# Asking for the first queries and keys ahead of every other transfer, in a scheduled attention and experts kernel

## The chip, the cores and the metric

The kernel runs on one core of a Trainium2 chip, as one program. The metric is the time of one execution in microseconds of device time, as the median of several runs; lower is better. The engines have short names: PE multiplies matrices, DVE, ACT and POOL are the vector, scalar and GpSimd engines, SP issues most of the transfers. Each engine runs its own list of instructions in order, and waits at an instruction for semaphores that others raise.

## What is computed

```python
def _attn_ref(q, k, v):                       # 4 batches, 8 heads, 576 rows, head size 64
    scores = scale * np.matmul(q, k.transpose(0, 1, 3, 2))
    kth = np.partition(scores, -32, axis=-1)[..., -32:-31]
    scores = np.where(scores >= kth, scores, -1e9)
    attn = softmax(scores)
    return np.matmul(attn, v)

def _moe_ref(x, modality_id, w_gate, modality_bias, w1, w2):   # 2304 tokens of 512
    e_idx = np.argmax(x @ w_gate + modality_bias[modality_id], axis=1)
    out[e_idx == e] = gate_w * (np.maximum(x @ w1[e], 0.0) @ w2[e])

def _moe2_ref(x, w_in, w_out, g_ln):          # w_in and w_out come as float64
    h = x @ w_in
    ln = layernorm(h * softmax(h)) * g_ln
    return ln @ w_out
```

Attention keeps the 32 largest scores of each row. Every token then goes to one of 8 experts, and after that through a dense block whose two weight matrices arrive as float64 numbers.

## The kernel before

**The work.** Attention goes through 4 batches of 5 query tiles: four of 128 rows and a short one of 64 (`t == 4`). Within a tile it goes through four pairs of heads. One head of one tile is a *unit* (a whole head pair for the short tile); there are 144. In a unit PE makes scores (L579), ACT copies them (L600, L610), DVE finds the 32nd largest with a run of maximum and replace steps (L612 to L629), ACT and POOL mask and take the exponential (L647 to L651). A `pair` then transposes the weights and multiplies them by the values (L664 to L742). After a tile, `route` and `place` count the tokens of each expert and scatter their numbers into a list in device memory, `idlist`, with an indirect transfer from POOL (L817). An expert slot (`front`, `back`) picks an expert, gathers token numbers (L884) and rows (L893), loads the expert's weights (L942, L945) and runs 128 tokens through them (L984, L1015); `moe2` does the dense block (L1036 to L1108).

**The float64 weights** come in 16 pieces. `doubles` loads one (L345) and rebuilds it as a float32 value and a remainder: ACT L346 and L355, POOL L348 and L357, DVE L349, L351 and L353. Three workers (`statics`) do this while attention runs. `consts` loads the token kinds, biases and gate weights (L294 to L301).

**What sets the order.** All of it is written as Python generators, which a small list scheduler (`Order`) plays at build time. A generator yields an `Op` (engine, assumed cost, the function that emits the instructions), a `get` or `put` of buffers, a `set` of an event, or an event that it waits for. The scheduler keeps a clock for each engine, picks the engine that can go first, and among the operations ready there the one with the best priority from the table `PRI`. So each engine's list of instructions is fixed when the program is built, and a small difference at its start can move many later choices. Nothing in the scheduler is a wait at run time; those are semaphores that the framework adds where one instruction needs another's result or buffer. An `Ev` is met once its time is set:

```python
        if isinstance(x, Ev):
            if x.t is None:
                return False
```

`load_k` asks for the keys of one head pair at a time (three transfers, L470 and L471, assumed cost 1900), `load_q` for the queries of a tile (L483, 530). Each has two buffers to begin with. `prep_kv` and `prep_q` transpose what has landed (L515, L522, L541) and split it in two parts (L490, L491). For a short query tile `prep_q` first writes zeros to two quarters of the tile with POOL (two instructions at L552).

Of the kernel before, what the change touches and what calls it, by code (L numbers as in the profile page):

```python
# [63 lines left out]
def tiles(b):  # L64


    return (4, 0, 1, 2, 3) if b < SHORT_FIRST else (0, 1, 2, 3, 4)


def rows_of(b, t):  # L70

    if t == 4:
        return (0 if b < SHORT_FIRST else 512), 64
    return t * 128 + (64 if b < SHORT_FIRST else 0), 128
# [125 lines left out]
def attn_moe_solu_kernel(ctx, tc, q, k, v, mid, w_gate, mbias, w1, w2, w_in, w_out, g_ln, out):  # L200
# [56 lines left out]
    def bc(ap, n, axis):  # L257
        shape = list(ap.shape)
        u = ap.unsqueeze(axis)
        shape.insert(axis, n)  # L260
        return u.to_broadcast(shape)
# [9 lines left out]
    def consts():  # L271


        yield "get", ("row", 2), ("xs", 1), ("B", 1)
        ta, tb = [sb.tile([128, NP * 144], F32, tag="row", name="cs", bufs=BUF["row"]) for _ in range(2)]
        tc_ = sb.tile([128, NP, 144], F32, tag="xs", name="cs", bufs=BUF["xs"])
        zl, bias2 = ta[:, 0:NLIST // 128].bitcast(I32), ta[:, 160:160 + B * NTILE * E].rearrange("p (i e) -> p i e", e=E)
        raw, rows = tb[0:32, 0:256].bitcast(I32), tb[0:64, 256:384]
        b01 = tc_[:, 0, 0:2 * E].rearrange("p (m e) -> p m e", e=E)
        mids = tc_[:, 1, 0:64]  # L280
        m32 = mid.bitcast(I32).rearrange("(n w) -> n w", w=2)

        def clear():
            nc.vector.memset(zl, 0)
            nc.vector.memset(raw, 0)
            nc.vector.memset(rows, 0.0)
            nc.vector.memset(iw, 0.0)

        yield Op("DVE", 1200, clear)

        def loads():
            for b in range(B):
                o4, o0 = b * S + rows_of(b, 4)[0], b * S + rows_of(b, 0)[0]
                nc.sync.dma_start(raw[4 * b:4 * b + 4, :], m32[o0:o0 + 512].rearrange("(t p) w -> t (p w)", p=128))  # L294
                nc.sync.dma_start(raw[4 * B + b:4 * B + b + 1, 0:128], m32[o4:o4 + 64].rearrange("(t p) w -> t (p w)", p=64))
            nc.sync.dma_start(rows[32:40, :], g_ln.rearrange("(k p) -> k p", p=128))
            nc.sync.dma_start(b01, bass.AP(tensor=mbias.tensor, offset=mbias.offset, ap=[[0, 128], [E, 2], [1, E]]))
            wgv = w_gate.rearrange("(p s d) e -> s d p e", s=2, d=D)
            for s in range(2):
                nc.sync.dma_start(iw[s * D:(s + 1) * D, :, 136 * s:136 * s + 8], wgv[s])  # L300
            nc.sync.dma_start(idlist.rearrange("(p c) o -> p (c o)", p=128), zl)  # L301

        t0 = yield Op("SP", 700, loads, lat=10000)

        def unit_rows():
            for s in range(2):
                r = slice(s * D, (s + 1) * D)
                nc.vector.tensor_copy(iw[r, :, 8 + s * D:8 + (s + 1) * D], bc(ident[r, s * D:(s + 1) * D], NP, 1))

        yield Op("DVE", 650, unit_rows, deps=[])  # L310
        yield Op("POOL", 330, lambda: nc.gpsimd.tensor_copy(rows[0:32], raw.rearrange("i (n w) -> i n w", w=2)[:, :, 0]), deps=[t0])
        pt = ps.tile([128, 64], F32, tag="B", name="pt", bufs=8)
        yield Op("PE", 60, lambda: nc.tensor.transpose(pt, rows, ident[0:64, 0:64]))
        yield Op("ACT", 250, lambda: nc.scalar.activation(mids, pt, AF.Copy))
        yield "put", ("B", 1)

        def biases():
            m, n = mids[:, 0:B * NTILE], mids[:, 32:32 + B * NTILE]
            nc.gpsimd.tensor_copy(g_sb, mids[:, 32:40])
            nc.gpsimd.tensor_scalar(n, m, -1.0, 1.0, op0=OP.mult, op1=OP.add)  # L320
            nc.gpsimd.tensor_tensor(bias, bc(n, E, 2), bc(b01[:, 0, :], B * NTILE, 1), op=OP.mult)
            nc.gpsimd.tensor_tensor(bias2, bc(m, E, 2), bc(b01[:, 1, :], B * NTILE, 1), op=OP.mult)
            nc.gpsimd.tensor_tensor(bias, bias, bias2, op=OP.add)

        yield Op("POOL", 1700, biases)
        yield "put", ("row", 2), ("xs", 1)
        yield "set", consts_done
# [125 lines left out]
    def after(n):  # L453
        if n:
            yield units_done[n]

    kraw, qraw = {}, {}
    k_loaded = {(b, p): Ev() for b in range(B) for p in range(NP)}
    q_loaded = {(b, t): Ev() for b in range(B) for t in range(NTILE)}

    def load_k():

        for b in range(B):
            for p in range(NP):
                yield "get", ("kr", 1)
                kr = kraw[b, p] = sb.tile([128, 10, D], F32, tag="kr", name="kr", bufs=BUF["kr"])

                def loads():
                    for s in range(2):
                        nc.sync.dma_start(kr[:, s:8:2, :], k[b, 2 * p + s, 0:512].rearrange("(p c) d -> p c d", c=4))  # L470
                    nc.sync.dma_start(kr[0:64, 8:10, :], k[b, 2 * p:2 * p + 2, 512:576, :].rearrange("s p d -> p s d"))  # L471

                t0 = yield Op("SP", 1900, loads, deps=[], lat=0)
                k_loaded[b, p].t = t0 + 3000
                yield "set", Ev()

    def load_q():
        for b in range(B):
            for t in tiles(b):
                r0, n = rows_of(b, t)  # L480
                yield "get", ("qr", 1)
                qr = qraw[b, t] = sb.tile([128, H, D], F32, tag="qr", name="qr", bufs=BUF["qr"])
                t0 = yield Op("SP", 530, lambda: nc.sync.dma_start(qr[:n], q[b, :, r0:r0 + n, :].rearrange("h p d -> p h d")),  # L483
                              deps=[], lat=0)
                q_loaded[b, t].t = t0 + 3000
                yield "set", Ev()

    def parts_of(hi, lo, pt, n):

# [745 lines left out]
    def statics(j):  # L1235

        steps = [(static_w_in, kk, i) for kk in range(KD) for i in range(2)]
        steps = ([(static_w_out, kk) for kk in range(KF)] + steps) if OUT_FIRST else (steps + [(static_w_out, kk) for kk in range(KF)])
        if j == 0:
            yield "get", ("xs", 1)  # L1240
            minus.append(sb.tile([128, NP * 144], F32R, tag="xs", name="minus", bufs=BUF["xs"])[:, 0:128])
            yield Op("ACT", 170, lambda: nc.scalar.activation(minus[0], ident, AF.Copy, scale=-1.0))
        for i in range(j, len(steps), WORKERS):
            yield from after(STATIC[i])
            yield from steps[i][0](*steps[i][1:], j)
        yield "set", in_done[j]
        if j == 0:
            yield from static_centre()
            for e in in_done:
                yield e  # L1250
            yield "put", ("xs", 1)
            yield "set", statics_done
# [158 lines left out]
    with tc.manual_schedule():  # L1411
        ord_.add(load_k(), pri("prep", 0))
        ord_.add(load_q(), pri("prep", 0))
        ord_.add(consts(), pri("const", 0))
        ord_.add(prep_k_all(), pri("prep", 0))
        ord_.add(prep_q_all(), pri("prep", 1))
        ord_.add(attention(), pri("unit", 0))
        for i in range(WORKERS):
            ord_.add(statics(i), pri("static", 0))
        ord_.add(slots(), pri("front", 0))  # L1420
        ord_.add(backs(), pri("ffn", 1))
        ord_.add(remains(), pri("ffn", 2))
        ord_.run()
# [60 lines left out]
```

## Time and profile before

| | us |
|---|---|
| median of 3 runs | 1048.77 |
| lowest and highest run | 1045.49, 1050.99 |
| the profiled execution | 1044.1 |
| its span, first to last instruction | 1042.3 |
| PE busy | 922.2 (88%) |
| DVE busy | 783.1 (75%) |
| ACT busy | 671.3 (64%) |
| POOL busy | 595.2 (57%) |

The shares are means over stages with different limits: DVE works nearly all the time while attention runs, to about 808 us, and little after it. Three views serve here. The windows view gives each engine's busy time in a stretch. The timeline lists instructions with their start and duration, and in brackets the idle time before one and what ended it. The chain of waits goes back from the last instruction to what released each step. A transfer appears with its issue on SPq or POOLq, or as a duration to its landing in the chain.

### The profile page before, as it was taken

To read this page: it belongs to the slowest core of one execution; us is meant where nothing else is said; L and a number is where in the kernel's file an instruction comes from. 1 tells how busy PE (TensorE), PEld (TensorE's weight loads), DVE (VectorE), ACT (ScalarE), POOL (GpSimd) and SP (SyncE) were. 2 spreads that over 40 slices of the span, in tenths; PEclk is the share of its full clock that TensorE was granted. 3 is DMA by queue.
4 is the path that set the end of the run, shared out by engine and by line. 5 is a ranking of instruction groups with operands and counts; after the bars stand their busy time and mean duration, and the time that the engine had idled before them with its cause. 6 is when DMAs were issued, how large, how long until landed. Compare 5 with 4: busy or idle time off the path is not lost.

```text
span 1042.3 us, 22339 instructions
## 1 busy us (share of the span) xinstructions
PE 922.2 (88%) x7150; PEld 758.6 (73%) x7150; DVE 783.1 (75%) x2474; ACT 671.3 (64%) x1688; POOL 595.2 (57%) x1334
## 2 busy tenths in 40 slices
PE   3867759998989899999999999999999989998983
PEld 2434536976768788787887878888788778887872
DVE  5999969997799999789999898999999224432001
ACT  3767748776677778777777778877776523433211
POOL 4667856656456776657486675666774536541201
PEclk7788878999999999999999999999999999999997
DMA  6524153544414354554444445344444566433440
GB/s 164 167 68 134 49 89 96 162 116 99 127 52 116 93 155 84 148 129 125 131 114 74 145 112 118 96 129 94 119 123 83 78 158 192 136 108 103 150 125 14
DMA packets 153752, 119.28 MB, mean 114 GB/s; under 512 B 48508, under 2 KB 126488, under 8 KB 153624
## 3 DMA queue, kind: packets, MB, share of 16 engines
q1 hardware_dynamic: 149528, 107.69, 40.1%
q0 software_dynamic: 4096, 10.05, 3.1%
q8 instruction: 59, 0.97, 0.4%
q14 instruction: 69, 0.57, 0.2%
HBM read 105.50 MB, written 12.21 MB: 113 GB/s over the span
## 4 chain that ended last, share of the span: by engine, by line
PE 41%; DVE 17%; POOL 9%; DMA 7%; ACT 7%; issue 5%; SPq 0%; POOLq 0%; ACTq 0%; DVEq 0%
PE py L1015 8%; PE ph L984 7%; PE po L1097 7%; DMA wraw<-in_moe_w_dram 5%; PE ph L1036 5%; DVE M L620 4%; PE po L717 4%; POOL e L649 3%; PE pt L683 3%; PE pS L579 2%; DVE tht L629 2%; PE pt L914 2%; PE px L726 1%; DVE M L612 1%; ACT e L648 1%
## 5 line engine op out<-in xcount | busy, mean ns | idle before, releaser
L649 POOL TENSOR_TENSOR e<-ss,e 128x576 f32<-128x576 f32 x144 | 204.7, 1424 | 51.7 <-ACT e L648 46.3
L984 PE MATMUL ph<-xT,wraw 128*128 128x128 f32 x1088 | 149.6, 282 | 9.7 <-DMA wraw<-in_moe_w_dram 9.5
L1015 PE MATMUL py<-hh,wraw 128*128 128x128 f32 x1088 | 148.6, 281 | 7.4 <-ACT hh L994 6.5
L984 PEld LDWEIGHTS ph<-xT,wraw 128*128 128x128 f32 x1088 | 136.4, 196 | 16.2 <-DMA wraw<-in_moe_w_dram 7.1
L651 ACT ACTIVATE e<-e,nb 128x576 f32<-128x576 f32 x144 | 111.6, 775 | 52.6 <-POOL e L649 51.3
L1015 PEld LDWEIGHTS py<-hh,wraw 128*128 128x128 f32 x1088 | 134.9, 195 | 13.3 <-ACT hh L994 8.3
L648 ACT ACTIVATE e<-ss,bt 128x576 f32<-128x576 f32 x144 | 111.2, 774 | 38.4 <-POOL bt L647 38.2
L620 DVE MATCH_REPLACE8 M<-tops,M 128x288 f32<-128x288 f32 x288 | 127.2, 443 | 0.0
L1097 PE MATMUL po<-wo,lT 128*128 128x512 f32 x432 | 119.9, 415 | 4.5 <-DVE lT L922 2.2
L717 PE MATMUL po<-eT,vt 128*64 128x128 f32 (+3 forms) x1600 | 116.5, 280 | 7.0 <-ACT eT L687 4.1
L1036 PE MATMUL ph<-wi,yT 128*128 128x512 f32 x432 | 115.1, 407 | 2.0 <-ACT yT L1203 1.9
L717 PEld LDWEIGHTS po<-eT,vt 128*64 128x64 f32 (+1 forms) x1600 | 84.0, 140 | 40.1 <-issue 15.5
L629 DVE MAX8 tht<-M 128x8 f32<-128x576 f32 x144 | 107.9, 750 | 0.6
L579 PE MATMUL pS<-kT,qT 64*128 64x288 f32 (+1 forms) x864 | 94.2, 322 | 13.5 <-ACT kT L490 5.0
L683 PE MATMUL pt<-identr,e 128*128 128x128 f32 (+1 forms) x640 | 95.3, 274 | 9.7 <-ACT wi L382 6.6
L687 ACT ACTIVATE eT<-pt 128x512 f32<-128x512 f32 (+1 forms) x160 | 88.1, 551 | 15.0 <-PE pt L683 13.0
L579 PEld LDWEIGHTS pS<-kT,qT 64*128 64x128 f32 (+1 forms) x864 | 72.1, 192 | 31.2 <-issue 8.2
L1097 PEld LDWEIGHTS po<-wo,lT 128*128 128x128 f32 x432 | 77.7, 192 | 23.1 <-DVE lT L922 4.2
L683 PEld LDWEIGHTS pt<-identr,e 128*128 128x128 f32 (+1 forms) x640 | 72.4, 144 | 26.3 <-issue 7.3
L1036 PEld LDWEIGHTS ph<-wi,yT 128*128 128x128 f32 x432 | 76.5, 188 | 20.2 <-ACT yT L1203 2.8
L994 ACT ACTIVATE hh<-ph 128x128 f32<-128x128 f32 (+1 forms) x144 | 40.1, 278 | 71.3 <-PE ph L984 63.4
L612 DVE TENSOR_TENSOR M<-pS,ss 128x288 f32<-128x288 f32 x144 | 64.5, 448 | 24.8 <-ACT ss L610 24.0
(218 smaller groups left out, 1819.6 us busy)
## 6 DMA issues: line engine op xcount, KB each, us to landing
wraw<-in_moe_w_dram SPq DMA_DIRECT2D x288, 256.0 KB
xrows<-xs SPq DMA_DIRECT2D x16, 288.0 KB
kr<-in_k_dram SPq DMA_DIRECT2D x32, 128.0 KB
qr<-in_q_dram SPq DMA_DIRECT2D x16, 256.0 KB
raw<-in_moe_w_out_dram SPq DMA_DIRECT2D x8, 512.0 KB
vt<-in_v_dram SPq DMA_DIRECT2D x32, 128.0 KB
raw<-in_moe_w_in_dram SPq DMA_DIRECT2D x8, 512.0 KB
wstage<-da SPq DMA_DIRECT2D x8, 256.0 KB
```

The costliest lines, as they stand in the source:

```text
L579: nc.tensor.matmul(bank[s][hf], x[r, a, p, :], kt[r, c, at:at + HALF], start=i == 0, stop=i == 2)
L620: nc.vector.match_replace(out=M, in_to_replace=rounds[r], in_values=M, imm_value=NEG)
L629: t0 = yield Op("DVE", 660, lambda: nc.vector.max(th, W), deps=[t0, tm])
L648: yield Op("ACT", 667, lambda: nc.scalar.activation(e, ss, AF.Relu, bias=bt, scale=-BIG))
L649: yield Op("POOL", 1360, lambda: nc.gpsimd.tensor_tensor(e, ss, e, op=OP.subtract))
L651: yield Op("ACT", 760, lambda: nc.scalar.activation(e, e, AF.Exp, bias=nb, scale=0.125, accum_out=z))
L683: nc.tensor.transpose(pt[:, c, :], ef[r, at:at + 128], ident[r, r])
L717: nc.tensor.matmul(po[hs, :n], w, x, start=c == 0, stop=c == 4)
L984: nc.tensor.matmul(ph[:, :n], a[:, kk * 128:(kk + 1) * 128], b[:, kk, c0:c0 + n], start=kk == 0 and i == 0, stop=kk == KD - 1 and i == len ...
L1015: nc.tensor.matmul(py[c // k_][:, c % k_, :n], a[:, c * 128:(c + 1) * 128], b[:, :n], start=first and m == 0 and c % k_ == 0 and i == 0, s ...
L1036: nc.tensor.matmul(ph, y[a][:, kk, :], wi[b][:, kk, i * 512:(i + 1) * 512], start=kk == 0 and j == 0, stop=kk == KD - 1 and j == 2)
L1097: nc.tensor.matmul(po, l[a][:, c, :], wo[b][:, kk, :], start=kk == 0 and j == 0, stop=kk == KF - 1 and j == 2)
```

## The change

A new event `begun` is set by the first query load. Until then `load_k` stops after its first head pair, `consts` stops before its loads, and the three workers stop before their first weight piece. Nothing else is edited.

```diff
--- before.py
+++ after.py
@@ -300,6 +300,7 @@
                 nc.sync.dma_start(iw[s * D:(s + 1) * D, :, 136 * s:136 * s + 8], wgv[s])
             nc.sync.dma_start(idlist.rearrange("(p c) o -> p (c o)", p=128), zl)
 
+        yield begun
         t0 = yield Op("SP", 700, loads, lat=10000)
 
         def unit_rows():
@@ -455,6 +456,8 @@
             yield units_done[n]
 
     kraw, qraw = {}, {}
+
+    begun = Ev()
     k_loaded = {(b, p): Ev() for b in range(B) for p in range(NP)}
     q_loaded = {(b, t): Ev() for b in range(B) for t in range(NTILE)}
 
@@ -472,6 +475,7 @@
 
                 t0 = yield Op("SP", 1900, loads, deps=[], lat=0)
                 k_loaded[b, p].t = t0 + 3000
+                yield begun
                 yield "set", Ev()
 
     def load_q():
@@ -483,7 +487,7 @@
                 t0 = yield Op("SP", 530, lambda: nc.sync.dma_start(qr[:n], q[b, :, r0:r0 + n, :].rearrange("h p d -> p h d")),
                               deps=[], lat=0)
                 q_loaded[b, t].t = t0 + 3000
-                yield "set", Ev()
+                yield "set", begun if begun.t is None else Ev()
 
     def parts_of(hi, lo, pt, n):
 
@@ -1240,6 +1244,7 @@
             yield "get", ("xs", 1)
             minus.append(sb.tile([128, NP * 144], F32R, tag="xs", name="minus", bufs=BUF["xs"])[:, 0:128])
             yield Op("ACT", 170, lambda: nc.scalar.activation(minus[0], ident, AF.Copy, scale=-1.0))
+        yield begun
         for i in range(j, len(steps), WORKERS):
             yield from after(STATIC[i])
             yield from steps[i][0](*steps[i][1:], j)
```

The scheduler then makes other choices. Both programs hold the same instructions, but for four head pairs whose last step is one DVE copy (L737) instead of two ACT copies (L732). From the 62nd of the 144 units to the end the lists of all engines are the same, instruction for instruction; ahead of that they differ. In the changed program a line number is 1 to 5 higher, by the lines added above it.

**First place: the start.** SP's transfers in the order before (`kr` keys, `qr` queries, `raw` a float64 weight piece, `vt` values), and then in the changed order:

```order
L470 DMA kr<-in_k_dram 128x4x64 x2
L471 DMA kr<-in_k_dram 64x2x64
L470 DMA kr<-in_k_dram 128x4x64 x2
L471 DMA kr<-in_k_dram 64x2x64
L483 DMA qr<-in_q_dram 128x8x64 x2
L345 DMA raw<-in_moe_w_out_dram 128x1024
L504 DMA vt<-in_v_dram 128x256 x2
L505 DMA vt<-in_v_dram 128x1x64
L345 DMA raw<-in_moe_w_out_dram 128x1024 x2
L483 DMA qr<-in_q_dram 128x8x64
```

```order
L473 DMA kr<-in_k_dram 128x4x64 x2
L474 DMA kr<-in_k_dram 64x2x64
L487 DMA qr<-in_q_dram 128x8x64
L473 DMA kr<-in_k_dram 128x4x64 x2
L474 DMA kr<-in_k_dram 64x2x64
L487 DMA qr<-in_q_dram 128x8x64
L346 DMA raw<-in_moe_w_out_dram 128x1024
L508 DMA vt<-in_v_dram 128x256 x2
L509 DMA vt<-in_v_dram 128x1x64
L487 DMA qr<-in_q_dram 128x8x64
L346 DMA raw<-in_moe_w_out_dram 128x1024 x2
```

The first query load (L483, now L487) moved ahead of the second head pair's keys, and the third ahead of two weight pieces; the first weight piece and the constants keep their place behind the first two query loads. On ACT the same stretch, before and then changed (`ss` a unit's score copy, `dd` and `dc` steps on a weight piece):

```order
L490 ACTIVATE qT<-pt 128x512
L490 ACTIVATE kT<-pt 128x512
L346 ACTIVATE dd<-raw 128x512
L490 ACTIVATE qT<-pt 128x512
L490 ACTIVATE kT<-pt 128x2x64
L346 ACTIVATE dd<-raw 128x512 x2
L355 ACTIVATE dc<-raw 128x512
L600 ACTIVATE ss<-pS 128x288 x2
```

```order
L494 ACTIVATE qT<-pt 128x512
L494 ACTIVATE kT<-pt 128x512
L494 ACTIVATE qT<-pt 128x512
L347 ACTIVATE dd<-raw 128x512
L494 ACTIVATE kT<-pt 128x2x64
L604 ACTIVATE ss<-pS 128x288
L347 ACTIVATE dd<-raw 128x512 x2
L356 ACTIVATE dc<-raw 128x512
L614 ACTIVATE ss<-pS 128x288
```

One score copy L600 (now L604) moved ahead of two L346 (now L347), which need weight pieces; the second one stays behind them.

**Second place: POOL at the first batch's short query tile.** `qT` is the query tile, `idlist` the list that the scatter writes; in brackets stand the semaphores that an instruction names, `DMASW` with a number for POOL's own transfers in turn, `Pool` for POOL's own instructions. Before, then changed:

```order
L552 TENSOR_TENSOR qT_1564<-onesf_81 64x8x64 [waits PE_49]
L798 TENSOR_SCALAR oh_1620<-w_1559,w8_1560 128x8 [waits DVE_49]
L649 TENSOR_TENSOR e_1590<-ss_1427,e_1590 128x576 [waits PE_49,Activation_49]
L357 TENSOR_TENSOR dc_1496<-dc_1496,dd_1497 128x512 [waits DMAHW6_49,DVE_49,Activation_49]
L816 CAST posi_1647<-pos_1646 128x1 [waits DMASW0_49,DVE_49]
L617 TENSOR_SCALAR nb_1594<-tops_1593 128x1
L817 DMA idlist_68<-tokid_87,posi_1647 18560x1 [waits Pool_49]
L552 TENSOR_TENSOR qT_1564<-onesf_81 64x8x64 [waits DMASW1_49,Pool_49]
L647 TENSOR_SCALAR bt_1544<-tht_1251 128x1 [waits DVE_49,Pool_49]
```

```order
L556 TENSOR_TENSOR qT_1600<-onesf_81 64x8x64 [waits PE_49]
L802 TENSOR_SCALAR oh_1647<-w_1586,w8_1587 128x8 [waits DVE_49]
L556 TENSOR_TENSOR qT_1600<-onesf_81 64x8x64 [waits DMASW0_49,Pool_49]
L653 TENSOR_TENSOR e_1620<-ss_1442,e_1620 128x576 [waits PE_49,Activation_49,Pool_49]
L820 CAST posi_1661<-pos_1660 128x1 [waits DVE_49]
L621 TENSOR_SCALAR nb_1617<-tops_1616 128x1
L821 DMA idlist_68<-tokid_87,posi_1661 18560x1 [waits Pool_49]
L651 TENSOR_SCALAR bt_1581<-tht_1264 128x1 [waits DVE_49]
```

The second L552 (now L556) moved from behind the scatter L817 (now L821) to ahead of it. It named the semaphore of the scatter just issued, `DMASW1`; now it names `DMASW0`, that of the first scatter, which stands 37 rows higher.

**Third place: POOL at the first expert slot.** L884 gathers token numbers, L893 (which names `DMASW2`, the semaphore of L884) gathers the rows. Before, then changed:

```order
L880 CAST li_1844<-idx_1802 128x2 [waits Pool_49]
L884 DMA ids_1884<-idlist_68,li_1844 128x1 [waits Pool_49]
L647 TENSOR_SCALAR bt_1688<-tht_1251 128x1 [waits DVE_49]
L617 TENSOR_SCALAR nb_1781<-tops_1780 128x1 [waits DVE_49]
L649 TENSOR_TENSOR e_1826<-ss_1536,e_1826 128x576 [waits Activation_49]
L893 DMA xg_1896<-xrows_66,ids_1884 128x576 [waits DMAHW7_49,DMAHW4_49,DMASW2_49]
```

```order
L884 CAST li_1841<-idx_1802 128x2 [waits Pool_49]
L888 DMA ids_1875<-idlist_68,li_1841 128x1 [waits DMASW1_49,Pool_49]
L621 TENSOR_SCALAR nb_1792<-tops_1791 128x1 [waits DVE_49]
L651 TENSOR_SCALAR bt_1684<-tht_1264 128x1 [waits DVE_49]
L897 DMA xg_1884<-xrows_66,ids_1875 128x576 [waits DMAHW5_49,DMAHW0_49,DMASW2_49]
```

Between the two gathers stood three instructions, one of them L649; now there are two short ones, and L649 moved behind. L884 (now L888) now names the scatter's `DMASW1` itself. Between that scatter and this L888 stand 18 instructions of POOL, two of them L649. In the next batch the second L556 names the row gather that stands five rows higher; its like before named an older output write.

The weight pieces moved as well: the last step on the 16th piece (L353) stands on DVE behind 23 units before, and now behind 18; that on the 8th behind 10, and now 9.

## Rows read from the trace of the kernel before

**Rows 1.** Windows: us, then busy us of each engine in that stretch, PE clock, DMA

```profile
20.00:146.00 126.00, 91.60 (x506) 56.90 (x504) 121.10 (x346) 89.93 (x208) 89.80 (x130) 0.80 0.36 109
146.00:156.00 10.00, 4.36 (x18) 2.16 (x16) 1.92 (x6) 1.21 (x4) 1.61 (x5) 0.67 0.70 33
156.00:182.00 26.00, 24.54 (x157) 16.83 (x157) 24.34 (x73) 20.97 (x50) 17.79 (x34) 0.88 0.32 101
182.00:372.00 190.00, 174.11 (x1467) 146.80 (x1467) 169.60 (x563) 139.65 (x363) 116.37 (x276) 0.96 0.40 106
372.00:808.00 436.00, 423.38 (x3624) 358.51 (x3622) 399.04 (x1310) 331.43 (x864) 283.24 (x668) 1.00 0.47 118
```

**Rows 2.** Timeline of DVE: the last search step of the 62nd unit (start us, us)

```profile
372.41 0.75 DVE L629 MAX8 tht<-M 128x8 f32<-128x576 f32 x1
```

**Rows 3.** Chain of waits, three transfers on it: start us, us, what

```profile
144.93 9.18 DMA idlist<-tokid,posi
...
207.04 4.10 DMA ids<-idlist,li
...
211.40 4.61 DMA xg<-xrows,ids
```

**Rows 4.** Timelines of POOL, DVE and PE from 144 to 157 us: the hole

```profile
144.93 1.10 POOL L817 DMA_INDIRECT idlist<-tokid,posi  x1 [0.17 <-POOL nb L617]
154.25 1.03 POOL L552 TENSOR_TENSOR qT<-onesf 64x512 fp32r<-64x512 f32 x1 [8.22 <-DMA idlist<-tokid,posi]
155.90 0.17 DVE L665 RECIPROCAL rz<-z 128x2 f32<-128x2 f32 x1 [8.08 <-POOL z L664]
156.94 1.11 PE L683 MATMUL pt<-identr,e 128*128 128x128 f32 x4 [6.57 <-ACT wi L382]
```

**Rows 5.** Timeline of the first 18 us, SP (issue), PE, ACT and DVE

```profile
2.80 1.28 SPq L470 DMA_DIRECT2D kr<-in_k_dram  x2
4.80 1.22 SPq L483 DMA_DIRECT2D qr<-in_q_dram  x2
8.48 1.08 PE L541 MATMUL pt<-identr,qr 128*128 128x128 f32 x4 [8.48 <-DMA qr<-in_q_dram]
14.32 0.68 ACT L346 ACTIVATE dd<-raw 128x512 f32<-128x512 f32 x1 [1.98 <-DMA raw<-in_moe_w_out_dram]
16.86 0.70 ACT L600 ACTIVATE ss<-pS 128x288 f32<-128x288 f32 x2
17.88 0.46 DVE L612 TENSOR_TENSOR M<-pS,ss 128x288 f32<-128x288 f32 x1 [2.94 <-ACT ss L610]
```

**Rows 6.** Timeline of POOL: the gathers of the first expert slot

```profile
168.06 1.09 POOL L884 DMA_INDIRECT ids<-idlist,li  x1 [0.29 <-POOL li L880]
172.24 1.03 POOL L893 DMA_INDIRECT xg<-xrows,ids  x1 [0.15 <-issue]
```

**Rows 7.** Groups by line: busy us, mean ns, then idle before it

```profile
L649 POOL TENSOR_TENSOR e<-ss,e 128x576 f32<-128x576 f32 x144 | 204.7, 1424 | 51.7 <-ACT e L648 46.3 <-PE py L1015 4.2
L647 POOL TENSOR_SCALAR bt<-tht 128x1 f32<-128x1 f32 x144 | 33.1, 230 | 78.8 <-DVE tht L629 62.6 <-DVE hnm L1045 2.3 <-PE px L726 2.3
L737 DVE TENSOR_TENSOR xs<-px,rz 128x144 f32<-128x144 f32 x33 | 9.7, 294 | 0.1
L351 DVE SCALAR_TENSOR_TENSOR da<-raw,dd 128x512 int32<-128x512 int32 x16 | 16.0, 1001 | 0.1
L353 DVE TENSOR_SCALAR dd<-da 128x512 int32<-128x512 int32 x16 | 10.1, 629 | 0.1
```

**Rows 8.** Two DVE steps on the weight pieces: duration min/median/max in ns

```profile
L351 DVE SCALAR_TENSOR_TENSOR da<-raw,dd x16: 665/686/2868, 13.8 to 161.8; 128x512 int32<-128x512 int32 x16
L353 DVE TENSOR_SCALAR dd<-da x16: 398/422/1553, 14.5 to 163.6; 128x512 int32<-128x512 int32 x16
```

**Rows 9.** Timeline of POOL and DVE at 129 us

```profile
128.75 1.41 POOL L649 TENSOR_TENSOR e<-ss,e 128x576 f32<-128x576 f32 x1
128.89 1.55 DVE L353 TENSOR_SCALAR dd<-da 128x512 int32<-128x512 int32 x1
```

## The prediction

> **What bounds the kernel now.** I read the stages first [rows 1]. From 20 to 146 us VectorE (DVE) is busy 121.10 of 126 us: the top-32 search sets the pace, and TensorE (PE) has only 91.60 us of work. From 156 to 182 us both are nearly full, from 182 to 372 us PE holds 174.11 of 190 us, and from 372 to 808 us 423.38 of 436. So the end is set by DVE first and by PE from about 182 us on. One stretch belongs to nobody: from 146 to 156 us DVE is busy 1.92 us of 10 and PE 4.36.
>
> Then I asked how far the change reaches. By the two orders the engines run the same instructions in the same sequence from the 62nd of the 144 units on; in the old trace that unit's last search step starts at 372.41 us [rows 2]. What the change gives or takes is decided before that, and then carried: PE is 97% busy for the 436 us that follow, so a shift found there should stand at the end. Its work up to there is the same in both programs.
>
> **The hole at 146 us** is read from the chain of waits and the engines' timelines [rows 3, 4]. On GpSimd (POOL) the scatter L817 (token numbers into `idlist`) starts at 144.93. The next instruction, the second L552 (zeros for a short query tile), starts only at 154.25, after 8.22 us idle that the trace puts down to that scatter, whose landing the chain shows as 9.18 us. L552 computes nothing from the scatter; the order shows the wait, `DMASW1`, the semaphore of the scatter just issued. Behind L552 stand the steps that free the units: DVE's L665 waits 8.08 us, PE's L683 6.57 us.
>
> **The change, part by part** (line numbers of before; the changed program's are up to 5 higher).
>
> *Start.* The first query load moves ahead of three key transfers on the SP queue. They took from 2.80 to 4.80 us [rows 5], so the query is asked for 2.00 us sooner, and PE, which sat 8.48 us on it, starts by so much earlier. What follows gives most of it back: ACT had the first score copy L600 at 16.86, behind weight steps L346 that waited for data (to 14.32, and once more). In the new order one L600 stands ahead of two of those L346, so DVE's first L612, which waited 2.94 us, can begin at once. But the second unit's L600 still stands behind both L346, and their two weight loads now stand behind the third query load on SP. I take 0.5 us of gain; the ends are 0 and 2.9. Constants and weights were behind the first queries already, so delaying them removes nothing.
>
> *The hole.* In the new order the second L552 stands one instruction after the first and ahead of the scatter, and the semaphore it names is that of the first scatter (`DMASW0`), 37 rows back. Nothing holds it. I take the whole DVE wait, 8.1 us; the other end is 0, if something else waits for the same landing.
>
> [...]
>
> *What is late next.* Three POOL waits come in its place [rows 3, 6, 7].
> - The first gather of token numbers, L884, must wait for that scatter's data. In the new order 18 instructions stand between them after the scatter's own 1.10 us: two L649 at 1.42 and sixteen short ones, about 0.23 each by L647: 7.6 us in all, against 9.18. The gaps between short ones fill most of the rest: 0.5 us, between 0 and 1.6.
> - Behind L884 the row gather L893 needs its landing. Before, three instructions stood between, one of them an L649, and it started at 172.24 with 0.15 us idle. Now two short ones do. The landing took 4.10 us in the next slot; less L884's 1.09 and two times 0.23, POOL stands still for 2.6 us. In that slot a like wait of 1.83 lay on the chain; I take half, 1.3, between 0 and 2.6.
> - In the next batch the second L552 names the L893 issued five rows ahead. That landing took 4.61; less L893's 1.03 and four short ones, 2.7 us. PE leads by then: 0.5, between 0 and 2.7.
>
> *Who writes the outputs.* Four head pairs change from two ACT copies to one DVE copy, L737: 4 x 0.294 = 1.2 us [rows 7]. DVE leads for about half of the units concerned: 0.6, between 0 and 1.2.
>
> All else in the first 372 us is a reshuffle without a sign that I can read: 0.
>
> **The sum:** -0.5 - 8.1 + 0.5 + 1.3 + 0.5 + 0.6 = -5.7 us. The profiled execution took 1044.1 us (span 1042.3 and 1.8 around it), so 1038.4; the median of the runs, 1048.8, lies 4.7 above that execution, so the forecast on its scale is **1043 us**. With every cost at its end: 1048.8 - 11.0 = 1038 and 1048.8 - 8.1 + 8.1 = 1049.
>
> **The rivals.**
> 1. *The hole only moves.* Another POOL step, L884 or a short one that names the new scatter, inherits the landing. For it: L884 is the one that needs the data, and my count leaves it little room. Against it: 7.6 us of work stand in between, where there was none. Without the 8.1 us the other terms leave +2.4: 1051 us.
> 2. *Slower: DVE's integer steps meet POOL.* Each of the 16 weight pieces has a step L351 and a step L353 on DVE. Their medians are 0.686 and 0.422 us, their means 1.001 and 0.629: 5.0 and 3.3 us lost over 16 each [rows 7, 8]. One meeting shows how [rows 9]: L353 at 128.89 took 1.55 us and ended with POOL's L649, which had begun at 128.75. The new order packs pieces 8 to 16 between units 9 and 18, before 10 and 23, where POOL does more for each piece. If 24 of the 32 steps met it as that one did (1.13 more each, 27.1 us, or 18.8 beyond today's 8.3), the forecast turns into 1043 + 19 = 1062. From 17 such steps on (19.2 us lost, which is 8.3 + 5.7 + 5.2) the kernel is slower than before by over 0.5%. Against it: most of the 32 run at their median now. [...]
> 3. *More gain: the experts start earlier and fill PE.* The last weight piece passes DVE at unit 18 instead of 23, so steps that wait for all weights can come sooner. PE idles 15.9 us from 182 to 372 [rows 1]; half of that back gives 1035 us. Against it: those idles are waits for data, which stay.
>
> **How the numbers follow.** About 0.5% (5.2 us) is what a measurement of this kernel can tell from no change, so faster means under 1043.6 and slower over 1054.0. The forecast gets 0.55, of which its own range, 1038 to 1049, puts 0.35 under 1043.6 and 0.20 inside. Rival 1 gets 0.17 (same), rival 2 0.13 (slower), rival 3 0.15 (faster). Faster 0.50, same 0.37, slower 0.13. The range goes from rival 3's 1035 to 1053, past rival 1; it leaves out most of rival 2 and what lies beyond rival 3.
>
> **What would show it.** In the new profile PE's first transpose starts near 6.5 us. No L556 (L552 before) waits 8 us for an `idlist` scatter, DVE has no idle of 8 us near 145 us, and POOL waits 2 to 3 us at the first row gather. The 62nd L633 (L629 before) starts near 367 us instead of 372.4, and the end moves by the same amount. If L888 or another POOL step waits over 5 us for the scatter, rival 1 holds; if the means of the two integer steps near twice their medians, rival 2; if PE idles under 9 us in the 190 us ahead of the 62nd unit, rival 3. I am wrong in kind if the shift at the 62nd unit is not the shift at the end.

## The result and the profile after

| | before | after |
|---|---|---|
| median of five runs each, us | 1048.27 | 1059.06 |
| the profiled execution, us | 1044.1 | 1059.5 |
| PE busy, us | 922.2 | 939.3 |
| DVE busy, us | 783.1 | 784.2 |

The changed kernel is slower: ratio 1.0113, 95% interval 1.0079 to 1.0147, about 12 us of loss, where the forecast was 6 us of gain and its range ended at 1053. One of the five changed runs, 1455.7 us at a granted clock of 0.561, is a slow execution and isn't in the ratio. Rival 2 had the sign, but not for its reason. The two profiled executions stand 15.4 us apart, more than the medians, because the one of before lies below its runs.

The same five stretches as in [rows 1], of the changed kernel:

```profile
20.00:146.00 126.00, 93.92 (x497) 57.46 (x496) 120.19 (x334) 86.67 (x198) 88.11 (x127) 0.82 0.35 105
146.00:156.00 10.00, 9.51 (x46) 6.28 (x43) 9.28 (x36) 8.03 (x19) 8.03 (x15) 0.71 0.63 82
156.00:182.00 26.00, 22.58 (x153) 15.41 (x151) 19.66 (x56) 14.82 (x37) 11.81 (x26) 0.87 0.56 127
182.00:372.00 190.00, 168.98 (x1371) 139.73 (x1368) 162.98 (x537) 134.48 (x346) 112.37 (x266) 0.92 0.36 98
372.00:808.00 436.00, 421.12 (x3595) 358.28 (x3595) 392.37 (x1295) 327.00 (x853) 282.96 (x669) 0.99 0.47 117
```

The second line is the place of the hole: DVE is busy 9.28 of 10 us, before 1.92. The third and the fourth give the gain back: DVE 19.66 against 24.34, then PE 168.98 against 174.11, at a clock of 0.92 against 0.96 and with 96 matmul records fewer.

**The hole is gone.** Timelines of POOL and DVE in the changed kernel (start us, us, instruction, in brackets the idle before it), to be held against [rows 4, 6]:

```profile
147.37 1.04 POOL L556 TENSOR_TENSOR qT<-onesf 64x512 fp32r<-64x512 f32 x1
150.39 1.09 POOL L821 DMA_INDIRECT idlist<-tokid,posi  x1 [0.16 <-POOL nb L621]
160.81 1.09 POOL L888 DMA_INDIRECT ids<-idlist,li  x1 [0.46 <-POOL li L884]
167.78 1.01 POOL L897 DMA_INDIRECT xg<-xrows,ids  x1 [4.53 <-DMA ids<-idlist,li]
167.23 0.69 DVE L429 TENSOR_TENSOR wo<-pw,wo 128x512 fp32r<-128x512 f32 x1 [3.87 <-ACT wo L428]
```

The second zero instruction waits for nothing, and the token gather L888 for 0.46 us. But the row gather L897 waits 4.53 us, and DVE stands 3.87 us at a centring step. SP's timeline shows what stood ahead of them; first of the changed kernel, then of before:

```profile
142.55 11.96 SPq L423 DMA_DIRECT2D wc<-wstage  x6
157.83 0.42 SPq L946 DMA_DIRECT2D wraw<-in_moe_w_dram  x1
...
160.12 0.59 SPq L946 DMA_DIRECT2D wraw<-in_moe_w_dram  x1
160.81 3.82 SPq L423 DMA_DIRECT2D wc<-wstage  x2
```

```profile
142.48 18.48 SPq L422 DMA_DIRECT2D wc<-wstage  x5
162.09 0.42 SPq L942 DMA_DIRECT2D wraw<-in_moe_w_dram  x1
...
166.55 0.44 SPq L422 DMA_DIRECT2D wc<-wstage  x1
```

The centring reads its weights back from DRAM (`wc`). In the changed order five expert loads of 256 KB are issued from 157.83 us on, two of the `wc` reads go behind them, and the gather of the token ids is issued together with those reads. The chain of waits has the read, and the list of transfers from 155 to 172 us has the landing of the ids; below it, the landing in the kernel before by the same list of the same stretch:

```profile
160.81 8.94 DMA wc<-wstage
```

```profile
wraw<-in_moe_w_dram SPq DMA_DIRECT2D x5, 256.0 KB
wc<-wstage SPq DMA_DIRECT2D x2, 256.0 KB
ids<-idlist,li POOLq DMA_INDIRECT x1, 6.7
```

```profile
ids<-idlist,li POOLq DMA_INDIRECT x1, 2.8
```

The ids took 6.7 us, against 4.10 in the slot of [rows 3] and 2.8 at this same place before. The number of transfers isn't the difference: before, too, five expert loads and two `wc` reads fall in the stretch. But there the gather (168.06) comes 1.5 us behind the last of them, and the DMA engines are busy 52% of its 2.8 us; in the changed kernel it comes with the last two, and they are busy 92% of its 6.7 us. That the backlog made it slow is a reading of the two traces; no run varied it alone.

**Where the units stand.** The n-th last search step (L629, L633 in the changed kernel) tells in every trace how far the work has come. The changed kernel's 62nd, for [rows 2]:

```profile
380.38 0.75 DVE L633 MAX8 tht<-M 128x8 f32<-128x576 f32 x1
```

The columns under numbers give the start of the n-th such step minus that in the trace of before, in us. "Stretch" is the longest time without an expert product (L984, L1015) between units 26 and 70, to about half a microsecond. Each lag is that of one execution, and 29 executions of before in one set lie between 1037.9 and 1054.6 us: a lag of 2 or 3 us alone says little.

| kernel | ratio to before, 95% | 24 | 26 | 36 | 62 | 65 | 81 | stretch |
|---|---|---|---|---|---|---|---|---|
| before | 1 | 0 | 0 | 0 | 0 | 0 | 0 | 26.3 |
| after | 1.0113 (1.0079 to 1.0147) | -4.6 | 0.4 | 3.3 | 8.0 | 12.7 | 15.7 | 50.9 |
| hole_only | 0.9968 (0.9944 to 0.9993) | -9.5 | -7.3 | -7.1 | -4.0 | -3.9 | -1.2 | 30.9 |
| start_again | 0.9991 (0.9971 to 1.0012) | 0.4 | 0.4 | 0.7 | 0.7 | 0.7 | 3.4 | |
| early_after | 0.9991 (0.9966 to 1.0016) | -4.7 | -0.8 | -0.1 | -2.4 | -2.4 | -1.9 | 26.4 |
| late_after | 1.0134 (1.0095 to 1.0173) | 0.6 | 2.0 | 6.5 | 8.3 | 12.7 | 16.7 | 50.8 |
| after_to_36 | 1.0032 (1.0010 to 1.0054) | -4.9 | 1.1 | 6.3 | 4.0 | 4.0 | 7.5 | 26.6 |
| after_from_36 | 1.0092 (1.0059 to 1.0125) | 0.4 | 0.4 | 0.8 | 3.6 | 7.8 | 11.5 | 51.3 |

The step of 2 to 4 us between units 80 and 81 isn't the change's: start_again and hole_only, whose engines run in the order of before there, have it too, and the one profile of before does not. PE waits there for an expert load (2.09 us in before, 3.08 in after).

### The profile page after: what moved, and what is told of

It is laid out like the page before. It is cut to its first block, busy times and chain, and to the rows that moved or that the text cites. A ratio compares the mean times of both kernels' runs of the same rounds, so it can differ in the third digit from the quotient of the medians.

```text
span 1057.7 us, 22329 instructions
## 1 busy us (share of the span) xinstructions
PE 939.3 (89%) x7150; PEld 769.4 (73%) x7150; DVE 784.2 (74%) x2478; ACT 670.1 (63%) x1680; POOL 595.4 (56%) x1334
## 4 chain that ended last, share of the span: by engine, by line
PE 45%; DVE 16%; POOL 10%; DMA 8%; ACT 7%; issue 6%; SPq 0%; POOLq 0%; ACTq 0%; DVEq 0%
PE py L1019 9%; PE ph L988 8%; PE po L1101 6%; PE po L721 5%; PE ph L1040 5%; DVE M L624 4%; PE pS L583 4%; DMA wraw<-in_moe_w_dram 4%; PE pt L687 3%; POOL e L653 3%; DMA ids<-idlist,li 2%; DVE tht L633 2%; PE pt L918 2%; DMA xg<-xrows,ids 1%; PE px L730 1%
## 5 line engine op out<-in xcount | busy, mean ns | idle before, releaser
L988 PE MATMUL ph<-xT,wraw 128*128 128x128 f32 x1088 | 152.4, 285 | 11.7 <-DMA wraw<-in_moe_w_dram 6.9
L1019 PE MATMUL py<-hh,wraw 128*128 128x128 f32 x1088 | 149.6, 283 | 7.2 <-ACT hh L998 6.5
L988 PEld LDWEIGHTS ph<-xT,wraw 128*128 128x128 f32 x1088 | 138.5, 198 | 18.9 <-DMA wraw<-in_moe_w_dram 5.2
L1019 PEld LDWEIGHTS py<-hh,wraw 128*128 128x128 f32 x1088 | 135.9, 196 | 12.8 <-ACT hh L998 8.3
L721 PE MATMUL po<-eT,vt 128*64 128x128 f32 (+3 forms) x1600 | 118.8, 283 | 5.5 <-ACT eT L691 3.8
L633 DVE MAX8 tht<-M 128x8 f32<-128x576 f32 x144 | 107.8, 749 | 0.6
L687 PE MATMUL pt<-identr,e 128*128 128x128 f32 (+1 forms) x640 | 97.8, 279 | 1.9 <-ACT eT L691 1.1
L687 PEld LDWEIGHTS pt<-identr,e 128*128 128x128 f32 (+1 forms) x640 | 74.7, 147 | 21.2 <-issue 9.9
```

The costliest lines, as they stand in the source:

```text
L633: t0 = yield Op("DVE", 660, lambda: nc.vector.max(th, W), deps=[t0, tm])
L687: nc.tensor.transpose(pt[:, c, :], ef[r, at:at + 128], ident[r, r])
L721: nc.tensor.matmul(po[hs, :n], w, x, start=c == 0, stop=c == 4)
L988: nc.tensor.matmul(ph[:, :n], a[:, kk * 128:(kk + 1) * 128], b[:, kk, c0:c0 + n], start=kk == 0 and i == 0, stop=kk == KD - 1 and i == len ...
L1019: nc.tensor.matmul(py[c // k_][:, c % k_, :n], a[:, c * 128:(c + 1) * 128], b[:, :n], start=first and m == 0 and c % k_ == 0 and i == 0, s ...
```

## The experiments

**1. The parts alone.** Two edits of the kernel before leave the planner's choices as they were. The first puts the two zero instructions together:

```diff
-                yield Op("POOL", 900, lambda: nc.gpsimd.tensor_tensor(z, o2, o2, op=OP.subtract), deps=[])
+            yield Op("POOL", 900, zeros, deps=[])
+            yield Op("POOL", 900, lambda: None, deps=[])
```

where `zeros` issues both halves. The second puts the first query load ahead, with the second key pair's transfers held until it is issued:

```diff
-                t0 = yield Op("SP", 1900, loads, deps=[], lat=0)
+                t0 = yield Op("SP", 1900, lambda: held.append(loads) if (b, p) == (0, 1) else loads(), deps=[], lat=0)
...
+                    while held:
+                        held.pop()()
```

hole_only:

> The kernel before with both zero instructions of a short query tile issued together, so that the second stands ahead of the scatter; the planner's order is otherwise that of before on every engine. If the hole is worth what the prediction took, the 8-us wait is gone, the 25th unit comes 8 us sooner and the time falls by about 8 us (1040 against 1048). Rival: the steps behind the hole (the centring of the output weights, the first gather) or the experts later on swallow it, and the time falls by 3 us or less.

Measured 0.9968 (0.9944 to 0.9993), 3.3 us of gain. In the trace the 23rd unit comes 8.7 us sooner and 7 to 8 us stand until unit 56; then 4.2 are lost by unit 60, where the fourth slot's first product comes only 3.5 us sooner (355.1 against 358.7). Its row gather waits 2.09 us for the ids where before had 0.75, and PE 3.66 for an output copy; timelines of POOL and PE in hole_only:

```profile
335.82 1.05 POOL L897 DMA_INDIRECT xg<-xrows,ids  x1 [2.09 <-DMA ids<-idlist,li]
344.18 0.85 PE L730 MATMUL px<-iw,oT 128*128 128x144 f32 x2 [3.66 <-ACT oT L728]
355.12 1.06 PE L988 MATMUL ph<-xT,wraw 128*128 128x128 f32 x8
```

So the term was right where it arose, and less than half of it reached the end. By the two theories, 8 us or 3 us and less, that is nearer the second.

start_only, and then start_again:

> The kernel before with only the first query load put ahead of the second key pair's transfers on the SP queue; all engines otherwise in the order of before. The prediction took 0.5 us of gain for it, with ends of 0 and 2.9: 1045 to 1048. If the early transfers collide with the second key pair, it could be up to 2 us slower.

> The kernel before with only the first query load ahead of the second key pair's transfers (in the earlier run of this edit the delayed transfers brought the third pair's keys, of the same size, into the second pair's tile; here they bring the second's). Ratio 0.997 to 1.001 as there, the first transpose near 6.4 us.

0.9989 (0.9964 to 1.0015) and 0.9991 (0.9971 to 1.0012): no difference that shows. (start_only works on wrong keys in one pair, as the second text says; start_again is the one to go by.) In the changed kernel too the first steps are earlier and the first search step hardly (for [rows 5]):

```profile
6.39 1.09 PE L545 MATMUL pt<-identr,qr 128*128 128x128 f32 x4 [6.39 <-DMA qr<-in_q_dram]
...
17.55 0.46 DVE L616 TENSOR_TENSOR M<-pS,ss 128x288 f32<-128x288 f32 x1 [2.38 <-ACT ss L614]
```

hole_and_start:

> The two parts of the change that the prediction gave a sign, without the reshuffle: the kernel before with both zeros together and with the first query load ahead of the second key pair, every engine else in the order of before. The sum of the two measured alone is -3.3 and -1.1 us: 1042 to 1044. If they share one cover, it is no better than the zeros alone, 1043 to 1045.

0.9973 (0.9936 to 1.0009): no better than the zeros alone.

**2. Which half of the order.** A planner's order can be recorded and replayed: the kernel takes the next step from a list instead of from the priorities.

```diff
+            if self.listed:
+                now = {t["name"]: t for t in ready}
+                i = next((i for i, n in enumerate(self.listed) if n in now), None)
+                th = now[self.listed.pop(i)]
...
```

The list also fixes which engine writes each output. At the 25th unit the two orders have done the same but for two steps, so they can be cut there and joined crosswise.

late_after:

> A recorded list fixes the order: that of the kernel before up to its 25th unit, that of the changed kernel from there on (at that point the two differ by two steps in what has been done). Theory: the loss lies behind the 25th unit, where the changed order runs the experts ahead of the units; then this kernel is as slow as the changed one or slower, 1058 to 1062. Rival: the loss needs what the changed order does before the 25th unit (denser weight pieces, centring late); then this one stands near 1048.

early_after:

> The other half: order of the changed kernel up to the 25th unit, that of the kernel before from there on. Theory: the two traces are level at that unit (the changed one 1.1 us ahead at the 25th, 0.4 behind at the 26th), so this kernel takes 1046 to 1049. Rival: the early part sows the loss; then 1056 or more.

1.0134 and 0.9991. The theory holds: the early half of the change, hole and all, comes out even (its 4.7 us at unit 24 shrink to 0.8 at unit 26; in its trace, too, the row gather waits 4.75 us there and a centring step 3.66), and the late half carries the loss. Cut once more, at the 36th unit:

after_to_36:

> A recorded list: the changed order up to the 36th unit, that of before from there on (the two differ there by eleven steps in what has been done). Theory (the loss comes where the experts have run ahead and wait for routed tokens, units 48 to 65): the changed order is 3 us late at the 36th unit and stays so, ratio 1.000 to 1.005. Rival (the loss is sown between units 25 and 36): 1.008 or more.

after_from_36:

> The other half: the order of before up to the 36th unit, the changed order from there on. Theory: it has the stretch in which the experts stand still from the 52nd to the 60th unit, so it loses most of the 12 us, ratio 1.007 to 1.013. Rival: 1.003 or less.

1.0032 and 1.0092: 3.4 and 9.6 us, together about the changed kernel's loss. About three quarters of it are made by the order behind the 36th unit.

**3. What happens there.** From 36 units on the changed order has PE take expert products sooner: at the 44th unit its trace has 296 matmul records of L988 and L1019, that of before 256, at the 52nd 384 against 328. Then none until the 60th (384 against 411). The fourth slot needs 704 routed tokens (`PLAN`); the scatter of that tile starts at 337.3 us against 326.1. The stretches without an expert product in the windows view, first of before, then of the changed kernel, with three pieces of its end and two behind it:

```profile
332.40:358.70 26.30, 23.07 (x168) 18.12 (x167) 24.17 (x79) 20.37 (x53) 21.09 (x51) 0.94 0.31 84
```

```profile
319.80:370.70 50.90, 38.95 (x271) 29.64 (x270) 46.27 (x157) 35.65 (x91) 35.81 (x84) 0.83 0.18 55
...
356.00:360.00 4.00, 1.62 (x17) 1.42 (x14) 3.33 (x9) 1.93 (x6) 2.13 (x6) 0.58 0.24 74
360.00:364.00 4.00, 2.10 (x10) 1.70 (x8) 1.93 (x8) 2.89 (x8) 3.59 (x10) 0.50 0.19 74
364.00:368.00 4.00, 3.15 (x20) 2.14 (x20) 3.97 (x16) 2.13 (x6) 2.71 (x7) 0.50 0.17 66
...
380.00:384.00 4.00, 1.36 (x12) 1.15 (x12) 3.46 (x13) 2.71 (x6) 2.45 (x8) 0.99 0.71 143
384.00:388.00 4.00, 4.00 (x25) 3.81 (x26) 3.09 (x10) 0.45 (x2) 2.25 (x5) 0.58 0.51 162
```

PE idles 11.9 us of the changed kernel's stretch (before 3.2 of its 26.3), and near 357 us its granted clock falls to 0.50 (0.80 from 356 to 357 us, 0.50 from 357 to 358). DVE is busy 46.27 of the 50.9 us. After the stretch the fourth slot's own loads are late: the chain has one that took 7.97 us, PE waits for it (busy 1.36 us of the four from 380 us on), and the next four have a granted clock of 0.58. Both falls stand behind a wait of PE; that the wait brings the fall is a reading of this trace, and no run varied such a wait alone. Ahead of the fall near 357 us PE waited 1.66 us for an ACT copy of an output, and for gathered rows, 2.38 us, only then:

```profile
375.62 7.97 DMA wraw<-in_moe_w_dram
```

```profile
355.22 0.51 PE L730 MATMUL px<-iw,oT 128*128 128x144 f32 x2 [1.66 <-ACT oT L728]
...
359.09 1.09 PE L918 MATMUL pt<-identr,xg 128*128 128x128 f32 x4 [2.38 <-DMA xg<-xrows,ids]
```

One regularity runs through the table: the lag at the 65th unit is that of the fourth slot's first expert product, to 0.8 us. That product comes 12.0 us later than before in after, 11.9 in late_after, 7.1 in after_from_36 and 4.1 in after_to_36, and 2.5 and 3.5 us sooner in early_after and hole_only. This points to the late start of that slot as the way by which the loss reaches the end; the times agree, but no run moved that start alone.

Three more runs tried to move the experts alone.

experts_early:

> A recorded list: the order of the kernel before throughout, but from the 25th to the 63rd unit the steps of the experts (their products, weight loads, activations) stand where the changed order has them, counted by units. Theory: the loss comes from experts that run ahead of the units and then have no routed tokens, so this kernel loses most of what the changed order loses from unit 25 on: 1055 to 1062. Rival: the loss is in the order of the other steps (units, pairs, routing, gathers); then 1045 to 1050.

experts_held:

> The counterpart: the changed order throughout, but from the 25th to the 63rd unit the steps of the experts are held to where the order of before has them, counted by units. Theory: most of the loss goes, 1045 to 1051. Rival: it stays, 1056 or more.

hold_third (`yield from after(44 if j == 2 else 0)` ahead of the slot's products):

> The changed kernel with one more wait in the planner: the products of the third expert slot begin only after the 44th unit. In the new plan the experts have done 32, 36, 47 and 53 of their products at units 48, 52, 56 and 60; in the changed order 41, 48, 48, 48; before 34, 40, 48, 51. Theory: at least half of the loss goes, ratio to before 0.998 to 1.006. Rival: held experts don't help, or the re-made order costs as much elsewhere, 1.010 or more.

1.0312 (1.0258 to 1.0365), 1.0404 (1.0343 to 1.0465) and 1.0220 (1.0176 to 1.0263): all far slower, so none tells the theories apart. Where the steps of two orders are mixed step by step, each queue holds instructions that wait for another's: in experts_held SP stands for PE to free expert buffers, by the view of waits from 260 to 420 us (in total, times, longest):

```profile
SPq L1035 <- PE ph L1074: 38.3, 2, 24.1
```

In hold_third PE only idles earlier: it has no expert product for 52.3 us from 266 us on, and again none for 13.9 us from 353 us on. Holding the experts back doesn't bring the tokens of the fourth slot sooner.

**4. Other reshuffles.** Two kernels of before with one number of the planner changed that says nothing of the chip: `1290` to `1291`, and `530` to `540`.

one_ns:

> The kernel before with one number of the planner changed by 1 ns that says nothing of the hardware (1290 to 1291 for the attention product); the order changes from the 50th step or so of units on. In its plan the experts have done 46 of their products at the 52nd unit (40 before, 48 in the changed order) and stand still until the 60th. Theory (an order in which the experts run ahead loses, whatever made it): 1052 to 1060. Rival: the loss belongs to the moved query load, and a change of 1 ns leaves the time within 3 us of before.

ten_ns:

> The kernel before with the planner's cost of a query load at 540 ns in place of 530; the order changes from the 12th step of TensorE on, for most of the program. In the plan the experts have done 43, 48, 48 and 55 of their products at units 48, 52, 56 and 60: ahead as in the changed order, but the fourth slot follows sooner. If being ahead costs only where it ends in standing still, the ratio is 1.000 to 1.006; if being ahead is itself the loss, 1.008 or more; if a reshuffle has no sign, anything from 0.99 to 1.02.

1.0160 (1.0106 to 1.0213) and 1.0044 (1.0023 to 1.0066). One nanosecond in a planner's cost does as much as the change under study. So a reshuffle of this program moves the time by amounts like the one to be explained. (The ratio of one_ns is to runs of before made beside it, whose median was 1058.1 us.) Whether the stretch is the cause they leave open. one_ns has a stretch of about 47 us, but its lag in the trace is the same at the 60th and the 65th unit, 5.6 and 5.5 us, and most of its loss comes later. ten_ns has one of 45.7 us, and goes from 7.3 us ahead of before at the 60th unit to 2.1 behind at the 65th, 9.4 us in all, as the changed kernel does from 3.6 to 12.7; but its fourth slot starts 11.6 us sooner than in before. Its ratio fits two of the three readings named beforehand.

**5. What sets the pace in the stretch.** The changed order from a list, with ten copies of transposed weights moved from ACT to DVE:

```diff
-            yield Op("ACT", 478 if k_ == 2 else 264, lambda: nc.scalar.activation(et, pt, AF.Copy))
+            def copied():
+                if 26 <= (b * NTILE + t) * NP + p < 31:
+                    nc.vector.tensor_copy(et, pt)
...
```

copies_on_dve (with 52 to 60, which run behind the stretch):

> The changed kernel's own order from a list, with one thing different: the two copies of transposed weights out of PSUM (eT) of the nine head pairs 52 to 60 run on DVE in place of ACT. In the 50.9 us in which the changed kernel issues no expert product, ACT idles 4.6 us, DVE 21.3, PE 11.9, and ten of these copies stand there at 0.59 us. Theory: without expert work ACT sets the pace and PE waits; 5.9 us of ACT work taken away shortens the stretch by 3 to 6 us, and the end comes sooner by about as much: ratio to before 1.004 to 1.009, against 1.011. Rival (the chain from unit to unit through POOL or DVE sets the pace, or the copies now hold DVE up): stretch within 1.5 us of 50.9, ratio 1.010 or more.

copies_in_stretch:

> As the run before it, but for head pairs 26 to 30: the earlier edit took pairs 52 to 60, whose copies run at 592 to 629 us, so it said nothing of the stretch at 320 to 371 us. The changed kernel's own order from a list; the ten copies eT of these five pairs run on DVE (idle 21.3 of the 50.9 us) in place of ACT (idle 4.6). Theory (without expert work ACT sets the pace): the stretch is shorter by 3 to 6 us and the 65th unit as much sooner; ratio about 0.004 under that of the unaltered list beside it. Rival (a chain between ACT, POOL and DVE sets the pace, or DVE's search steps are held up): stretch within 1.5 us of 50.9, no gain.

changed_from_list:

> The changed kernel's own order from a list and nothing else: the reference for the run beside it. Ratio to before 1.008 to 1.015, as measured for the changed kernel; the stretch 50.9 us.

The expectations read the windows' columns one off. The 4.6 us of idle are DVE's, the 21.3 those of PE's weight loads; ACT idles 15.3. So the runs put work on the engine that was already the fullest, and that is a test too. The stretch of the list alone (changed_from_list), then with the copies (copies_in_stretch):

```profile
318.10:369.40 51.30, 39.44 (x275) 30.02 (x274) 46.65 (x158) 36.19 (x94) 36.12 (x86) 0.83 0.18 54
```

```profile
317.80:372.60 54.80, 41.02 (x275) 31.29 (x274) 51.15 (x166) 32.59 (x87) 36.36 (x86) 0.81 0.17 51
```

DVE has 4.5 us more to do, ACT 3.6 less, and the stretch is 3.5 us longer: DVE sets its pace, not ACT. Eight of the ten copies fall in it; one takes 0.68 us on DVE and about 0.59 on ACT, so that the slower copy itself makes under 1 us of the 3.5. The 65th unit comes 3.1 us later than in the list alone, so what is added to the stretch stands behind it. Ratios: 1.0096 (1.0071 to 1.0121) for the list alone, which is the changed kernel's within the noise, and 1.0167 (1.0137 to 1.0196) with the copies, about 7 us more (the intervals leave room for 2 to 13). The copies of later pairs gave 1.0157 (1.0115 to 1.0198) and say nothing of the stretch, which stayed at 51.1.

The same edits on the kernel with the zeros together rested on the same misreading:

hole_copies:

> The kernel before with both zeros together (0.997 alone) and the same eighteen copies on DVE. Its stretch without expert products is 30.9 us long, with ACT idle 6.2, DVE 11.6, PE 6.5 us. Theory: 1 to 3 us more gain, ratio 0.993 to 0.996. Rival: no more than the zeros alone, 0.997 or above.

hole_copies_in_stretch:

> The kernel before with both zeros together and the ten copies of head pairs 26 to 30 on DVE. Its stretch without expert products was 30.9 us. Theory: 1 to 3 us more gain than the zeros alone (0.997): 0.993 to 0.996. Rival: 0.997 or above.

0.9978 (0.9950 to 1.0006) and 0.9987 (0.9966 to 1.0008): no gain over the zeros alone. That kernel, at 0.9968, is the one that beats both.

## Why the prediction was wrong

- *Start*: right in size. First transpose at 6.39 us (6.5 said), nothing measurable at the end. DVE's first search step didn't "begin at once", though: it still stood 2.38 us for the second score copy, and came 0.33 us sooner.
- *The hole*: right in place, cause and size (8.1 taken, 8.7 at the 23rd unit when removed alone), wrong in what of it lasts. 3.3 us came to the end in hole_only; in the changed order it was level by the 26th unit.
- *L884 behind the scatter*: the number is right, 0.46 us of wait against 0.5, the reason only in part. The trace puts the 0.46 down to POOL's own step ahead, as it does the 0.29 of before; L888 stands 10.4 us behind the scatter, whose landing had taken 9.18 us before, and no POOL wait for it shows, so the landing was covered whole. Rival 1 fails with it: no POOL step waits over 5 us there.
- *L893 behind L884*: mis-sized. Taken as 1.3, at most 2.6; it was 4.53. The upper end rested on a landing of 4.10 us in another slot; this one took 6.7, issued 3 us behind the first of five expert loads. The same loads stood ahead of two `wc` reads, which the working never looked at.
- *The second L552 of the next batch*: inside its ends. 0.5 us was taken, 2.7 at most; it stood idle 1.55 us to 359.12, where the row gather ahead of it had landed at 358.95 (the trace names a DVE step instead).
- *Rival 2*: its own test fails, the means, 0.924 and 0.612 us below, are far from twice the medians of before. (In the meeting it showed, L353 ended 0.28 us behind L649, not with it.) Groups of DVE in the changed kernel, for [rows 7]:

```profile
L352 DVE SCALAR_TENSOR_TENSOR da<-raw,dd 128x512 int32<-128x512 int32 x16 | 14.8, 924 | 0.2
L350 DVE TENSOR_SCALAR dd<-dd 128x512 int32<-128x512 int32 x16 | 12.4, 772 | 4.7 <-POOL dd L349 4.7
L354 DVE TENSOR_SCALAR dd<-da 128x512 int32<-128x512 int32 x16 | 9.8, 612 | 0.1
L741 DVE TENSOR_TENSOR xs<-px,rz 128x144 f32<-128x144 f32 x37 | 10.8, 292 | 0.2 <-PE px L730 0.2
```

  The two steps it named took 24.6 us, before 26.1. L350, which it did not name, rose from 8.2 to 12.4 us.
- *Rival 3*: its sign fails too. PE idles 21.0 us in the 190 us ahead of the 62nd unit, where under 9 was asked for.
- *Who writes the outputs*: 37 against 33 copies of L741, 1.1 us of DVE's time, as said; what they cost at the end no run shows.
- **"All else in the first 372 us is a reshuffle without a sign that I can read: 0"** is the step that failed. It put at nothing, without bounds in the range, what turned out to be the largest piece of the change: the order behind the 25th unit alone lost 14 us (late_after, 1.0134), and that behind the 36th alone 9.6 (after_from_36, 1.0092). The two orders could have shown beforehand that the expert products come earlier against the units and then stop, but not what that would cost.
- *"A shift found there should stand at the end"*: wrong too, and by the sign that the prediction had set itself ("wrong in kind if the shift at the 62nd unit is not the shift at the end"). The same order isn't the same state. The changed kernel reaches the 62nd unit 8.0 us late and the 65th 12.7: PE waits there for the late loads of the fourth slot (busy 1.36 us of four) and then runs at a granted clock of 0.58, as the windows from 380 to 388 us show.

What stays open is how the 9.6 us behind the 36th unit divide between the long stretch and the rest of that order. The stretch is there in after, late_after and after_from_36 and absent in early_after and after_to_36; one_ns and ten_ns have one too, and their loss isn't told by it. copies_in_stretch lengthened it and lost more; no run shortened it under an otherwise unchanged order.

## What to carry over

Where a planner sets the order, a small edit is two changes: its local effect, and a new draw of everything behind. Price the second as a term of its own, with bounds from neutral edits (here 1 ns in one cost gave 1.6%, 10 ns in another 0.4%, both slower), before trusting the first. To have the local gain without the draw, move the instruction by hand under an unchanged order, and to find a loss, record both orders and join them crosswise where they have done the same work.

## What was not expected of the hardware

- The same gather of 128 token ids landed in 2.8 us at this place before, in 4.10 in the slot of [rows 3], and in 6.7 in the changed kernel, where the DMA engines were busy 92% of that time.
- An idle of PE of 3.08 us for an expert load, where before had 2.09, was followed by 2 us at a granted clock of 0.50; PE in the changed kernel, then in before:

```profile
485.25 1.16 PE L988 MATMUL ph<-xT,wraw 128*128 128x128 f32 x8 [3.08 <-DMA wraw<-in_moe_w_dram]
486.24 1.84 PE L1019 MATMUL py<-hh,wraw 128*128 128x128 f32 x8
```

```profile
471.18 1.16 PE L984 MATMUL ph<-xT,wraw 128*128 128x128 f32 x8 [2.09 <-DMA wraw<-in_moe_w_dram]
472.18 1.06 PE L1015 MATMUL py<-hh,wraw 128*128 128x128 f32 x8
```

The same eight matmuls (L1019, L1015) took 1.84 against 1.06 us. The granted clock from 487 to 489 us is 0.50; before, behind its wait, it is 1.00 from 471 to 475 us. The wait is 1 us longer, and between the 80th and the 81st unit the lag grows by 2.9.
